# A short last row tile of an expert, packed by GpSimd and run with 16 matmuls

## The chip, the cores and the metric

The kernel runs on one core of a Trainium2 chip. The metric is the device time of one execution in microseconds, the median of several runs. A core has five engines with a queue each: TensorE (matmuls, "PE" in the profile), VectorE ("DVE"), ScalarE ("ACT"), GpSimd ("POOL") and SyncE ("SP", which here only issues DMAs). They meet through semaphores.

## The reference

Chunked attention with memory tokens, then a mixture of experts over its output. Only the second half matters here:

```python
# x: (3072, 512), the attention's output; E = 8 experts, F = 1024, capacity = 768
logits = x @ w_gate
expert_idx = np.argmax(logits, axis=1)
gate_w = softmax(logits)[np.arange(N), expert_idx]
# rows of an expert, in order, up to the capacity
h = np.maximum(np.einsum('ecd,edf->ecf', disp, w1), 0.0)   # layer 1
y = np.einsum('ecf,efd->ecd', h, w2)                       # layer 2
out[i] = gate_w[i] * y[expert_idx[i], pos[i]]
```

Each row goes to one expert. With the inputs drawn here the eight experts get 529, 195, 426, 381, 565, 320, 162 and 494 rows. All arrays are float32.

## The kernel before

**Stages.** The attention runs first, over 24 tiles of 128 tokens. While it runs, the routing gives each token a slot in a DRAM table `x_d`, sorted by expert, and scatters the token's row there (512 values, its gate weight in column `D`, its token number in column `D + 1`). After it the experts run one after the other, in `expert(e)`, L933.

**Precision.** A float32 matmul is done as three matmuls in the fast format float32r: each operand is split into a part `hi` and a rest `lo`, and hi x hi, hi x lo and lo x hi are added in PSUM. So weights (`w1`, `w2`), rows (`x`) and the hidden layer (`h`) each exist twice. The splits are an ACT copy (`hi`) and a DVE subtraction (`lo`).

**Tiles of rows.** An expert has up to six tiles of 128 rows. Tiles 0 and 1 (`TA = 2` of them, "early" tiles) are used only by an expert with more than 512 rows (`big`), and by expert 0, whose first 256 rows are computed ahead while the routing ends. Tiles 2 to 5 (`TB = 4`) hold the other rows: tile `TA`, that is 2, always runs; tiles 3, 4 and 5 run if the count of rows says so. `m32` is the count in units of 32 rows, without the early ones. The counts are known only on the chip: engines load them into registers (`values`, L795) and branch with `tc.If`.

**One expert**, in the order in which each engine's queue has it:

1. SP: `load_x(e + 1)` (L813) loads the next expert's rows from `x_d` to `xg`, under a Switch over the number of tiles.
2. Layer 1 (`layer1`, L876): one of six variants by width, the next of which is announced by `hint`. TensorE fills PSUM banks `p1[0..3]` in turn, with 12 matmuls for each of 8 `f`; `relu` (L870) makes `hhi` on ACT and `hlo` on DVE. Between, `split2` splits w2, and SP then loads the next expert's `w2` (L957).
3. Layer 2 of tile `TA` on TensorE: `mm2` (L909), for each of 8 `f` three matmuls of 128x512, 24 in all. Among them stand the transposes of the next expert's rows (`trans_x`, L831).
4. `split1(3)`: three of the eight splits of the next expert's `w1`; then `put_y` (L914) of tile `TA`: DVE scales the PSUM bank by the gate weights into a buffer `y`, of which there are three in turn, and GpSimd issues an indirect DMA that scatters the 128 rows into the output.
5. `trans_a(e + 1)`, tiles 0 and 1 if the expert is big, and tiles 3, 4 and 5 under an If each (L982). Between them stand the other five splits of w1. An If that is not taken does one tiny matmul on TensorE instead (`instead`, L865).
6. SP: the load of `w1` of expert `e + 2` (L988) into `raw1`, once the eight splits have read it. The next expert's `load_x` stands behind it on SP's queue.

PSUM has eight banks: `p1[0..3]`, two more of `p2`, and two for the transposes. Layer 2 takes the banks by `order` (L764): tile 2 the first of `p2`, tile 0 the second, and tiles 1, 3, 4, 5 the banks `p1[0]` to `p1[3]`.

Of the kernel before, what the change touches and what calls it, by code (L numbers as in the profile page):

```python
# [10 lines left out]
I32 = mybir.dt.int32  # L11
# [39 lines left out]
class Kernel:  # L51
# [7 lines left out]
    def run(self):  # L59
        tc, nc = self.tc, self.nc  # L60
        with ExitStack() as ctx:
            wp = ctx.enter_context(tc.tile_pool(name="wp", bufs=1))
            dr = ctx.enter_context(tc.tile_pool(name="dr", bufs=1, space=bass.MemoryType.DRAM))
            self.x_d = dr.tile([E * self.nt * P, XW], F32, name="x_d")
            self.ident = wp.tile([P, P], F32, name="ident")
            make_identity(nc, self.ident)
            self.w1hi = wp.tile([P, KD, F], F32R, name="w1hi")
            self.w1lo = wp.tile([P, KD, F], F32R, name="w1lo")
            self.raw1 = wp.tile([P, KD, F], F32, name="raw1")
            self.raw2 = wp.tile([P, KF, D], F32, name="raw2")  # L70
            self.pad = wp.tile([P, XW], F32, name="pad")
            nc.vector.memset(self.pad[:, 0:260], 0.0)
            nc.gpsimd.memset(self.pad[:, 260:], 0.0)
            nc.gpsimd.memset(self.pad[:, D + 1:D + 2], BIG)
            self.pads = wp.tile([P, E], I32, name="pads")
            self.zb = wp.tile([P, P], BF16, name="zb")

            self.big = wp.tile([1, E], I32, name="big")
            self.m32 = wp.tile([1, E], I32, name="m32")
            self.kind = wp.tile([1, E], I32, name="kind")  # L80
            self.wide = wp.tile([1, E], I32, name="wide")
            flags = wp.tile([1, 2], I32, name="flags")
            self.full, self.ok = flags[:, 0:1], flags[:, 1:2]
            with tc.manual_schedule(engines={ET.PE, ET.Activation, ET.DVE, ET.Pool, ET.SP}):
                self.attention()
                self.experts(ctx)
# [620 lines left out]
    def finish_routing(self):  # L707
# [26 lines left out]
        nc.vector.tensor_scalar(out=ci, in0=self.m32, scalar1=1.0, scalar2=-1.0, op0=ALU.max, op1=ALU.add)  # L734
        nc.vector.tensor_scalar(out=ci, in0=ci, scalar1=2, scalar2=None, op0=ALU.logical_shift_right)
        nc.vector.scalar_tensor_tensor(out=self.kind, in0=self.big, scalar=float(TB), in1=ci, op0=ALU.mult, op1=ALU.add)
# [7 lines left out]
        top = sm.tile([1, 1], F32, name="f_top")  # L744
# [4 lines left out]
    def experts(self, ctx):  # L749
# [9 lines left out]
        self.my = ctx.enter_context(tc.tile_pool(name="my", bufs=3, side="right"))  # L759
        p1 = ctx.enter_context(tc.tile_pool(name="p1", bufs=1, space=PSUM))  # L760
# [3 lines left out]
        self.order = [TA] + list(range(TA)) + list(range(TA + 1, TA + TB))  # L764
# [14 lines left out]
        self.rows = self.values(self.kind, ET.SP, 3 * TB)  # L779
        self.load_x(0)  # L780
# [65 lines left out]
    def trans_a(self, e):  # L846
        with self.tc.If(self.a[e] > 0) as c:  # L847
            for d in range(0, KD, 2):
                self.trans_x(e, d, 2)
        self.instead(c, self.p2[1])  # L850
# [71 lines left out]

    def tokens(self, e, t0, t1):
# [4 lines left out]
    def layer2(self, e, t, tok):  # L928
        ps = self.p2[self.order.index(t)]
# [3 lines left out]
    def expert(self, e):  # L933
# [5 lines left out]
        if not e:  # L939
# [6 lines left out]
            ps = self.p2[self.order.index(TA - 1)]  # L946
# [18 lines left out]
        if e + 1 < E:  # L965
            self.hint(e + 1)

# [5 lines left out]
        self.put_y(e, self.p2[0], TA, tok)  # L973
        if e + 1 < E:
# [5 lines left out]
        self.instead(c, self.p2[1])  # L980
        split1(2)
        for t in range(TA + 1, TA + TB):  # L982
            with tc.If(m > 4 * (t - TA)) as c:
                self.layer2(e, t, tok)
            self.instead(c, self.p2[self.order.index(t)])
# [31 lines left out]
```

## Time and profile before

| what | us |
|---|---|
| median of 3 runs | 504.53 (504.53, 510.5, 504.26) |
| the profiled execution | 508.52 |
| its span, first to last instruction | 506.7 |
| TensorE busy in the span | 461.3 |
| VectorE busy | 295.4 |
| ScalarE busy | 233.8 |
| GpSimd busy | 115.4 |
| mean granted TensorE clock | 0.977 |

The span falls into the attention, until about 150 us, the routing and early tiles, and the experts, from about 190 us to the end. TensorE is the busiest engine; matmuls overlap, so that a row's time can exceed the time from its start to the next one's. In the timelines below a row has its start, its time, engine, line, operation, the tiles written and read, and in brackets the idle time of the engine just before it and what ended that. "issue" in that place means that the profile shows no releaser. "SPq", "DVEq" and so on are the sequencers of the engines.

### The profile page before, as it was taken

The numbers are of one execution on the slowest core, as the hardware profiler recorded it, in microseconds if no ns is written. First come the engines' busy times: TensorE is split into PE (matmuls) and PEld (weight loads), VectorE is DVE, ScalarE is ACT, GpSimd is POOL, SyncE is SP. The second block draws the span as 40 slices with busy tenths as digits, with TensorE's granted clock in tenths as the row PEclk, the third lists the DMA queues.
The fourth block names the chain that finished last, engine by engine and source line by source line (L and its number), as shares of the span: only waits on it lengthen the run. The fifth ranks groups of instructions, "written<-read, shape, count | busy, mean of one in ns | idle before, by whom it ended". The sixth has DMA issues, their size and how long they took to land.

```text
span 506.7 us, 11689 instructions
## 1 busy us (share of the span) xinstructions
PE 461.3 (91%) x4317; PEld 394.1 (78%) x4317; DVE 295.4 (58%) x678; ACT 233.8 (46%) x462; POOL 115.4 (23%) x151
## 2 busy tenths in 40 slices
PE   7889988998868599898999999999999999889993
PEld 6778776777558579787888899799988989767782
DVE  6899797999854723456555525726442565554410
ACT  6799778888432413325434314524330553433300
POOL 8531133554623370020100210010022011020011
PEclk9999999999997899999999999999999999989997
DMA  9697899974672585227472480543321644630010
GB/s 212 152 213 157 198 272 261 208 200 104 134 273 93 177 303 169 108 70 266 160 243 61 156 294 15 190 154 125 125 87 50 217 172 167 225 115 2 4 41 38
DMA packets 77816, 78.71 MB, mean 155 GB/s; under 512 B 31762, under 2 KB 58510, under 8 KB 77648
## 3 DMA queue, kind: packets, MB, share of 16 engines
q1 hardware_dynamic: 72848, 61.93, 42.6%
q0 software_dynamic: 4800, 14.95, 7.7%
q8 instruction: 55, 0.90, 0.8%
q14 instruction: 113, 0.93, 0.6%
HBM read 60.86 MB, written 15.99 MB: 152 GB/s over the span
## 4 chain that ended last, share of the span: by engine, by line
issue 37%; DMA 34%; PE 16%; DVE 7%; ACT 2%; SPq 2%; POOLq 1%; DVEq 0%; POOL 0%; ACTq 0%
DMA out_dram<-y,tok 27%; DMA x_d<-pad,pads 4%; PE ps L509 3%; PE ps L463 3%; PE ps L550 3%; PE ps L533 2%; ACT kw L480 2%; DVE vw L415 1%; PE ps L332 1%; PE ps L475 1%; PE ps L603 1%; DMA raw<-in_q_dram 1%; DMA vw<-in_v_dram 1%; SPq L397 1%; DMA xg<-x_d 1%
## 5 line engine op out<-in xcount | busy, mean ns | idle before, releaser
L912 PE MATMUL p<-w2hi,hhi 128*128 128x512 f32 x224 | 92.7, 414 | 6.5 <-ACT w2hi L854 5.1
L872 ACT ACTIVATE hhi<-p 128x384 fp32r<-128x384 f32 (+2 forms) x68 | 33.7, 497 | 140.2 <-PE p L863 118.1
L919 POOL DMA_INDIRECT out_dram<-y,tok x28 | 32.0, 1144 | 279.1 <-DVEq L847 142.3
L912 PE MATMUL p<-w2lo,hhi 128*128 128x512 f32 x224 | 89.1, 398 | 0.0
L912 PE MATMUL p<-w2hi,hlo 128*128 128x512 f32 x224 | 88.7, 396 | 0.0
L873 DVE SCALAR_TENSOR_TENSOR hlo<-p,hhi 128x384 fp32r<-128x384 f32 (+2 forms) x68 | 37.6, 564 | 70.6 <-ACT hhi L872 47.0
L863 PE MATMUL p<-xhi,w1hi 128*128 128x256 f32 (+5 forms) x288 | 57.6, 322 | 4.1 <-issue 2.5
L863 PE MATMUL p<-xlo,w1hi 128*128 128x256 f32 (+5 forms) x288 | 57.2, 321 | 0.0
L863 PE MATMUL p<-xhi,w1lo 128*128 128x256 f32 (+5 forms) x288 | 57.1, 321 | 0.0
L912 PEld LDWEIGHTS p<-w2hi,hhi 128*128 128x128 f32 x224 | 42.9, 191 | 15.0 <-ACT w2hi L854 5.3
L918 DVE TENSOR_SCALAR y<-p,xg 128x512 f32<-128x512 f32 x28 | 21.0, 749 | 56.7 <-PE p L912 33.9
L912 PEld LDWEIGHTS p<-w2hi,hlo 128*128 128x128 f32 x224 | 42.7, 191 | 10.1
L863 PEld LDWEIGHTS p<-xhi,w1hi 128*128 128x128 f32 x288 | 45.3, 189 | 6.7 <-issue 3.2
L912 PEld LDWEIGHTS p<-w2lo,hhi 128*128 128x128 f32 x224 | 42.9, 192 | 7.8
L863 PEld LDWEIGHTS p<-xlo,w1hi 128*128 128x128 f32 x288 | 46.2, 190 | 2.1
L863 PEld LDWEIGHTS p<-xhi,w1lo 128*128 128x128 f32 x288 | 46.0, 189 | 2.0
L843 ACT CAST xhi<-px 128x512 fp32r<-128x512 f32 x34 | 19.8, 587 | 49.4 <-PE px L839 28.2
L855 DVE TENSOR_TENSOR w2lo<-raw,w2hi 128x512 fp32r<-128x512 f32 x64 | 41.2, 687 | 0.7
L480 ACT COPY kw<-ps 64x256 f32<-64x256 f32 x92 | 35.7, 388 | 10.8 <-PE ps L475 9.6
L844 DVE TENSOR_TENSOR xlo<-px,xhi 128x512 fp32r<-128x512 f32 x34 | 23.4, 691 | 28.1 <-ACT xhi L843 23.7
L829 DVE TENSOR_TENSOR w1lo<-raw,w1hi 128x512 fp32r<-128x512 f32 x56 | 36.6, 686 | 2.5 <-ACT w1hi L828 1.3
L550 PE MATMUL ps<-vw,pT 128*32 128x130 f32 x768 | 29.4, 277 | 8.4 <-issue 4.7
(156 smaller groups left out, 712.9 us busy)
## 6 DMA issues: line engine op xcount, KB each, us to landing
raw<-in_moe_w_dram SPq DMA_DIRECT2D x16, 2048.0 KB
raw<-in_q_dram SPq DMA_DIRECT2D x11, 512.0 KB
raw<-in_k_dram SPq DMA_DIRECT2D x10, 512.0 KB
vw<-in_v_dram SPq DMA_DIRECT2D x57, 64.0 KB
xg<-x_d SPq DMA_DIRECT2D x3, 792.0 KB
vw<-in_v_dram SPq DMA_DIRECT2D x31, 72.0 KB
xg<-x_d SPq DMA_DIRECT2D x4, 528.0 KB
xg<-x_d SPq DMA_DIRECT2D x2, 1056.0 KB
```

The costliest lines, as they stand in the source:

```text
L480: (nc.vector.tensor_copy if n == 0 and i else nc.scalar.copy)(out=kw[r, 2 * i:2 * i + 2, :, hf, 24 + j:56:2], in_=ps[j * 64:j * 64 + 64, h ...
L550: nc.tensor.matmul(ps[32 * c4:32 * c4 + 32, i * 130:i * 130 + 130], pT[:, pr * P + 32 * c4:pr * P + 32 * c4 + 32], vw[:, c + c4 + 1, :, pr ...
L829: (eng or self.nc.vector).tensor_tensor(out=lo[sl], in0=raw[sl], in1=hi[sl].bitcast(F32), op=ALU.subtract)
L843: nc.scalar.copy(out=self.xhi[:, d:d + k, sl], in_=pv)
L844: nc.vector.tensor_tensor(out=self.xlo[:, d:d + k, sl], in0=pv, in1=self.xhi[:, d:d + k, sl].bitcast(F32), op=ALU.subtract)
L855: self.nc.vector.tensor_tensor(out=self.w2b[j // 4][:, j % 4], in0=self.raw2[:, j], in1=self.w2a[:, j].bitcast(F32), op=ALU.subtract)
L863: self.nc.tensor.matmul(ps, a[:, d, fs], b[:, d, o:o + w], start=(i + d == 0), stop=(i == 2 and d == KD - 1))
L872: self.nc.scalar.activation(out=self.hhi[hs], in_=ps, func=AF.Relu)
L873: self.nc.vector.scalar_tensor_tensor(out=self.hlo[hs], in0=ps, scalar=0.0, in1=self.hhi[hs].bitcast(F32), op0=ALU.max, op1=ALU.subtract)
L912: self.nc.tensor.matmul(ps, a[:, f, t * P:t * P + P], b, start=(f == 0 and i == 0), stop=(f == KF - 1 and i == 2))
L918: nc.vector.tensor_scalar(out=y, in0=ps, scalar1=self.xg[e % 2][:, t, D:D + 1], scalar2=None, op0=ALU.mult)
L919: nc.gpsimd.indirect_dma_start(out=self.out[:, :], out_offset=bass.IndirectOffsetOnAxis(ap=tok[:, t:t + 1], axis=0), in_=y, in_offset=None ...
```

## The change

A tile is *short* if it is the last one of tiles 3, 4 and 5 in use and holds at most 64 rows (counted in units of 32). A new array `last`, worked out beside `m32` in the routing, holds its number (1 to 3 for tiles 3 to 5) or 0, and PE, DVE and GpSimd load it into registers. With it:

- `pack`, on GpSimd, after layer 1 and ahead of tile `TA`'s scatter: it copies `hhi` of the 64 rows to the first 64 columns of the place of tile 5, and `hlo` of the same rows to the next 64 columns; the gate weights twice, and the token numbers. A nest of Ifs picks the tile.
- `layer2_short`, right behind tile `TA`: 128 packed columns against `w2a` (hi) and `w2b` (lo), 16 matmuls in place of 24. DVE scales the lower half into `z`, then the upper half and adds `z` to it; GpSimd scatters 64 rows.
- Tiles 3 to 5 run in their old place only if they have more than 64 rows, and the unpacked tile's Ifs stay.
- Banks: tiles 0, 1, 3, 4 get `p1[0]`, `p1[1]`, `p1[2]`, `p1[3]`, tiles 2 and 5 the first of `p2`, the short tile the second. The matmul of an untaken If goes to `p1[0]`.
- `top` in the routing takes the place of a dead row, which spares some memory.

```diff
+            self.last = wp.tile([1, E], I32, name="last")
...
         nc.vector.tensor_scalar(out=ci, in0=self.m32, scalar1=1.0, scalar2=-1.0, op0=ALU.max, op1=ALU.add)
+        left = late
+        nc.vector.tensor_scalar(out=left, in0=ci, scalar1=3, scalar2=None, op0=ALU.bitwise_and)
+        nc.vector.tensor_scalar(out=left, in0=left, scalar1=2.0, scalar2=None, op0=ALU.is_lt)
         nc.vector.tensor_scalar(out=ci, in0=ci, scalar1=2, scalar2=None, op0=ALU.logical_shift_right)
+        nc.vector.tensor_tensor(out=self.last, in0=ci, in1=left, op=ALU.mult)
...
-        self.order = [TA] + list(range(TA)) + list(range(TA + 1, TA + TB))
+        self.bank = [2, 3, 0, 4, 5, 0]
...
+        self.short = self.values(self.last, ENGS, TB)
...
+    def pack(self, e):
+
+        n, h, s = self.short[e], P // 2, (TA + TB - 1) * P
+        st, sg = self.my.tile([P, 1], I32, name="stok", bufs=2), self.my.tile([P, 1], F32, name="sgate", bufs=2)
+        xg, copy = self.xg[e % 2], self.nc.gpsimd.tensor_copy
+
+        def go(k):
+            if k < TB - 1:
+                with self.tc.If(n > k) as c:
+                    go(k + 1)
+                with c.Else():
+                    move(TA + k)
+            else:
+                move(TA + k)
+
+        def move(t):
+            if t * P < s:
+                copy(out=self.hhi[:, :, s:s + h], in_=self.hhi[:, :, t * P:t * P + h].bitcast(F32))
+            copy(out=self.hhi[:, :, s + h:s + P], in_=self.hlo[:, :, t * P:t * P + h].bitcast(F32))
+            for r in (0, h):
+                copy(out=sg[r:r + h, :], in_=xg[0:h, t, D:D + 1])
+            copy(out=st[0:h, :], in_=xg[0:h, t, D + 1:D + 2])
+
+        with self.tc.If(n > 0):
+            go(1)
+        return st, sg
+
+    def layer2_short(self, e, st, sg):
+
+        nc, h, s, ps = self.nc, P // 2, (TA + TB - 1) * P, self.p2[1]
+        for f in range(KF):
+            for i, b in enumerate((self.w2a[:, f], self.w2b[f // 4][:, f % 4])):
+                nc.tensor.matmul(ps, self.hhi[:, f, s:s + P], b, start=(f == 0 and i == 0), stop=(f == KF - 1 and i == 1))
+        y, z = self.my.tile([P, D], F32, name="y"), self.z
+        nc.vector.tensor_scalar(out=z, in0=ps[h:P, :], scalar1=sg[h:P, :], scalar2=None, op0=ALU.mult)
+        nc.vector.scalar_tensor_tensor(out=y[0:h, :], in0=ps[0:h, :], scalar=sg[0:h, :], in1=z, op0=ALU.mult, op1=ALU.add)
+        nc.gpsimd.indirect_dma_start(
+            out=self.out[:, :], out_offset=bass.IndirectOffsetOnAxis(ap=st[0:h, :], axis=0),
+            in_=y[0:h, :], in_offset=None, bounds_check=NTOK - 1, oob_is_err=False)
...
         if e + 1 < E:
             self.hint(e + 1)
+        st, sg = self.pack(e)
...
         self.put_y(e, self.p2[0], TA, tok)
+        with tc.If(self.short[e] > 0) as c:
+            self.layer2_short(e, st, sg)
+        self.instead(c, self.p2[2])
         if e + 1 < E:
             self.trans_a(e + 1)
...
         for t in range(TA + 1, TA + TB):
-            with tc.If(m > 4 * (t - TA)) as c:
+            with tc.If(m > 4 * (t - TA) + 2) as c:
                 self.layer2(e, t, tok)
-            self.instead(c, self.p2[self.order.index(t)])
+            self.instead(c, self.p2[2])
             split1(1)
```

More of the change, by code (lines that the diff above doesn't have):

```diff
@@ L742, in finish_routing @@
             nc.vector.scalar_tensor_tensor(out=self.wide, in0=self.m32, scalar=float(w // 32), in1=self.wide, op0=ALU.is_gt, op1=ALU.add)
-        top = sm.tile([1, 1], F32, name="f_top")
+        top = late[:, 0:1]
         nc.vector.tensor_reduce(out=top, in_=n[0:1, :], axis=AX.X, op=ALU.max)
@@ L759, in experts @@
         self.my = ctx.enter_context(tc.tile_pool(name="my", bufs=3, side="right"))
+        self.z = mr.tile([P // 2, D], F32, name="z")
         p1 = ctx.enter_context(tc.tile_pool(name="p1", bufs=1, space=PSUM))
@@ L849, in trans_a @@
                 self.trans_x(e, d, 2)
-        self.instead(c, self.p2[1])
+        self.instead(c, self.p2[2])
     def split2(self, todo):
@@ L928, in layer2 @@
     def layer2(self, e, t, tok):
-        ps = self.p2[self.order.index(t)]
+        ps = self.p2[self.bank[t]]
         self.mm2(ps, t, range(KF))
@@ L945, in expert @@
                     self.layer2(e, t, tok)
-            ps = self.p2[self.order.index(TA - 1)]
+            ps = self.p2[self.bank[TA - 1]]
             for i, fs in enumerate((range(0, 3), range(3, 6), range(6, KF))):
@@ L979, in expert @@
                 self.layer2(e, t, tok)
-        self.instead(c, self.p2[1])
+        self.instead(c, self.p2[2])
         split1(2)
         for t in range(TA + 1, TA + TB):
-            with tc.If(m > 4 * (t - TA)) as c:
+            with tc.If(m > 4 * (t - TA) + 2) as c:
                 self.layer2(e, t, tok)
-            self.instead(c, self.p2[self.order.index(t)])
+            self.instead(c, self.p2[2])
             split1(1)
```

## The prediction, before the changed kernel was timed

> **What bounds the kernel now.** I read the page's head first, then the TensorE timeline of the expert stage, then the list of what TensorE waited for, then the DVE, GpSimd and SyncE timelines around each wait.
>
> ```profile
> span 506.7 us, 11689 instructions
> PE 461.3 (91%) x4317; PEld 394.1 (78%) x4317; DVE 295.4 (58%) x678; ACT 233.8 (46%) x462; POOL 115.4 (23%) x151
> 212.69 0.19 PE L868 MATMUL p<-zb 128*128 128x2 bf16 x2
> 223.89 0.18 PE L868 MATMUL p<-zb 128*128 128x2 bf16 x1
> 223.93 0.73 PE L863 MATMUL p<-xhi,w1hi 128*128 128x256 f32 x4
> 239.38 0.63 PE L839 MATMUL px<-ident,xg 128*128 128x128 f32 x4 [2.42 <-issue]
> 254.07 1.05 PE L863 MATMUL p<-xhi,w1hi 128*128 128x448 f32 x4 [0.31 <-DVE y L918]
> 437.50 0.63 PE L839 MATMUL px<-ident,xg 128*128 128x128 f32 x4 [1.52 <-issue]
> 451.86 1.16 PE L863 MATMUL p<-xhi,w1hi 128*128 128x512 f32 x4 [2.51 <-issue]
> ```
>
> Inside the expert stage TensorE runs nearly without holes. Between the two L868 markers at 212.69 and 223.89 lie two layer 2 tiles of expert 0, 48 matmuls in 11.20 us: 0.233 us each (the 0.4 us "busy" of one overlaps its neighbours). The marker itself, the matmul of an If not taken, costs 0.04 us (223.89 to 223.93). So TensorE sets the time, except in four places of the expert stage shown above. Two of them, 2.42 us in expert 1 and 1.52 us in expert 6, matter here. They are the first transposes of the *next* expert's rows: the wait is for a load.
>
> ```profile
> 225.47 0.37 SPq L988 DMA_DIRECT2D raw<-in_moe_w_dram  x1
> 232.71 0.37 SPq L825 DMA_DIRECT2D xg<-x_d  x1
> 424.50 0.37 SPq L988 DMA_DIRECT2D raw<-in_moe_w_dram  x1
> 431.61 0.37 SPq L825 DMA_DIRECT2D xg<-x_d  x1
> 237.00:238.00 1.00, 0.00 (x0) 0.00 (x0) 0.89 (x2) 0.09 (x1) 0.00 (x0) 1.00 0.35 124
> 238.00:239.00 1.00, 0.00 (x0) 0.00 (x0) 0.00 (x0) 0.00 (x0) 0.00 (x0) 1.00 0.08 31
> ```
>
> The last two rows are windows in expert 1 (their last two columns are the DMA share and GB/s): the DMA engines run dry while TensorE idles, and then it starts. The row load is issued 7.2 us (225.47 to 232.71) and 7.1 us (424.50 to 431.61) after the weight load w1 on the same queue, and TensorE starts 13.9 us (225.47 to 239.38) and 13.0 us (424.50 to 437.50) after that weight load. So in these two experts the clock of everything is the moment at which SyncE may issue L988, and that is when the eighth split of w1 has been done on DVE.
>
> ```profile
> 215.91 0.75 DVE L918 TENSOR_SCALAR y<-p,xg 128x512 f32<-128x512 f32 x1
> 216.94 1.42 POOL L919 DMA_INDIRECT out_dram<-y,tok  x1 [9.38 <-DVEq L847]
> 220.60 0.75 DVE L918 TENSOR_SCALAR y<-p,xg 128x512 f32<-128x512 f32 x1 [1.26 <-DMA out_dram<-y,tok]
> 221.27 0.68 DVE L829 TENSOR_TENSOR w1lo<-raw,w1hi 128x512 fp32r<-128x512 f32 x1
> 224.09 0.75 DVE L918 TENSOR_SCALAR y<-p,xg 128x512 f32<-128x512 f32 x1 [2.13 <-PE p L868]
> 224.76 0.68 DVE L829 TENSOR_TENSOR w1lo<-raw,w1hi 128x512 fp32r<-128x512 f32 x1
> 216.94 3.54 DMA out_dram<-y,tok
> 371.32 3.33 DMA out_dram<-y,tok
> 375.43 0.97 POOL L919 DMA_INDIRECT out_dram<-y,tok  x1 [2.69 <-DMA out_dram<-y,tok]
> 206.59 2.69 DMA out_dram<-y,tok
> ```
>
> This is expert 0, whose tiles are TA, t3 and t4 (TA+1, TA+2 are called t3, t4 here). The second output tile of DVE (220.60) waits until the first one's scatter has landed (216.94 + 3.54 = 220.48): three buffers y go round, and t3 comes three allocations after TA. And GpSimd's second scatter of a chain (375.43, expert 4) waits until the first has landed (371.32 + 3.33 = 374.65), and starts 0.78 us later: scatters to the output go one at a time.
>
> **The change part by part.**
>
> *Fewer matmuls.* By the reference's counts (529, 195, 426, 381, 565, 320, 162, 494 rows) the last tile has 64 rows or fewer in experts 0, 2, 4, 5 and 6. Each replaces 24 matmuls by 16: 8 x 0.233 = 1.87 us, in all 9.33 us, every one on TensorE's path. In experts 1, 3 and 7 nothing is saved.
>
> *The pack on GpSimd.* Two copies of 128x512 (one in expert 2) and three of 64x1.
>
> ```profile
> L829 POOL TENSOR_TENSOR w1lo<-raw,w1hi 128x512 fp32r<-128x512 f32 x8 | 10.5, 1307 | 17.8 <-ACT w1hi L828 17.8
> L496 POOL COPY kw<-kw 64x672 f32<-64x672 f32 x10 | 7.4, 739 | 40.5 <-ACT kw L480 17.9 <-PE ps L642 9.0 <-DVE m L517 7.4
> L542 POOL COPY xr<-tok 128x1 f32<-128x1 f32 x24 | 5.5, 240 | 0.2
> 405.02 0.56 DVE L873 SCALAR_TENSOR_TENSOR hlo<-p,hhi 128x384 fp32r<-128x384 f32 x1 [1.20 <-ACT hhi L872]
> 411.73 0.19 PE L868 MATMUL p<-zb 128*128 128x2 bf16 x2
> ```
>
> A copy of 672 elements takes 739 ns, the two-input operation on 512 takes 1307 ns: 0.6 to 1.3 us each, so 1.2 to 2.6 us for both; the three small ones at 240 ns (0.7 us) follow them, and TensorE doesn't need them. In expert 5 the last hlo ends at 405.58, tile TA's matmuls at 411.73: 6.1 us of cover, and GpSimd is idle then. I cost it at nothing; without cover it would be 2.6 us. In expert 0 GpSimd is held until 206.59 + 0.97 by an early scatter, and TA ends at 212.69: 5.1 us of cover. The Trainium skill ("SBUF — State Buffer", section on who interferes with whom) adds that a GpSimd operation reading SBUF and a DVE operation with two SBUF inputs lock each other out for a whole instruction; as an estimate by that page the two copies could each wait for one DVE split (0.68 us above), 4.0 us in all and still under cover, and nothing in this trace shows such a wait.
>
> *DVE.* A short tile takes two operations (z, y) of about 0.75 us in place of one. DVE is at 58%, so this costs nothing by itself. But they stand on DVE's queue ahead of five splits of w1, and they wait for TensorE's short tile.
>
> *Scatters and buffers: what is queued behind.* Now y is taken by TA, short, t0, t1, t3: t3 comes three after *short*. In expert 0, from TA's end at 212.69: y(TA) ends at 216.66, its scatter is issued at 216.94 and lands at 220.48. The short tile's matmuls end at 216.4, z and y by 218.3, but its scatter starts only 0.78 us after that landing, 221.26, and lands after 2.69 to 3.54 us (the extremes above; I take 3.1, the middle), at 224.36. TensorE has finished t3 at 212.69 + 40 x 0.233 = 222.0, but y(t3) starts at 224.48; then come 0.67 to the next operation, split seven (0.68), 0.16 of branch and split eight (0.68): L988 at 226.7. It was 225.47. So although TensorE is 1.87 us ahead, the loads are 1.2 us *later*, and expert 1's transposes start 1.2 us later than now. Expert 5 is alike:
>
> ```profile
> 414.95 0.75 DVE L918 TENSOR_SCALAR y<-p,xg 128x512 f32<-128x512 f32 x1
> 415.98 3.18 DMA out_dram<-y,tok
> ```
>
> landing 419.16, short's scatter 419.94 to 423.04, y(t3) 423.17, L988 at 425.4 in place of 424.50: 0.9 us later. The price is (1.87 + 1.2) + (1.87 + 0.9) = 5.84 us. With the quickest scatters it is 5.0, with the slowest 6.7; without the buffer wait 1.9. In experts 2, 4 and 6 no such load is in the way: 4 ends in t3, whose buffer is long free because t0 and t1 lie between; 2 has t4 after t3 and 17 us of layer 1 behind it; 6 loads nothing more.
>
> *The clock.* The two waits grow to 2.42 + 3.07 = 5.5 us and 1.52 + 2.77 = 4.3 us.
>
> ```profile
> 237.85:241.27 3.42, 1.90 (x11) 1.62 (x12) 0.82 (x3) 0.59 (x1) 0.00 (x0) 1.00 0.57 163
> 449.48:452.89 3.41, 1.03 (x5) 0.89 (x6) 1.29 (x3) 0.00 (x0) 0.01 (x1) 1.00 0.23 84
> 452.89:456.30 3.41, 3.41 (x10) 2.65 (x9) 1.01 (x2) 0.00 (x0) 1.16 (x1) 0.50 0.06 23
> ```
>
> Windows of 3.41 us, the granted clock in the third column from the end: a window in which TensorE was busy for 1.90 us did no harm, one with 1.03 us was followed by 3.41 us at half clock, a loss of 1.7 us. A hole of 4.3 us leaves, whatever its place, a window with at most 1.3 us of work, nearer to the second. I take 1.7 us for each: 3.4 us; the bounds are 0 and two windows each, 6.8.
>
> *Banks.* t3 moves from the bank that layer 1's second f uses to that of its third: the 0.31 us at 254.07 goes.
>
> *Small things.* Eight more untaken Ifs on TensorE at 0.04 us: 0.3. Eight more register values on TensorE, DVE and GpSimd:
>
> ```profile
> 177.09 1.09 DVE L773 MEMSET p<- 128x256 f32 x4
> 179.80 0.17 DVE L925 CAST tok<-xg 128x2 int32<-128x2 f32 x1 [1.62 <-issue]
> 165.68 0.35 DVE L735 TENSOR_SCALAR f_ci<-f_ci 1x8 int32<-1x8 int32 x1
> 171.49 0.43 DVE L343 SCALAR_TENSOR_TENSOR hlo<-ps,hhi 128x256 fp32r<-128x256 f32 x1 [2.69 <-ACT hhi L342]
> ```
>
> 33 values are loaded within 1.62 us, so 8 take at most 0.4; I count it all. Three more DVE operations in the routing, at most 0.35 us each, vanish in the 2.69 us for which DVE then waits anyway.
>
> *Sum:* -9.33 + 5.84 + 3.4 - 0.31 + 0.3 + 0.4 = +0.3 us. The profiled execution took 508.52 us (span 506.7), 4 us above the median of the runs shown, 504.53; I put the difference on the median: 504.8 us.
>
> **The rivals.** *Everything arrives.* If the scatters or buffers don't hold the splits (by a quicker landing, or because y(t3) needn't wait), 9.33 us less 0.3 for the small things: 495.5 us. Against it stand 220.60 and 375.43, which show both waits. *Late loads, no clock loss:* 504.8 - 3.4 = 501.4; for it, that 2.42 us of idle in expert 1 cost no clock.
>
> *New stalls at branches (slower).* TensorE's hole of 2.51 us at 451.86 stands at the jump into expert 7's widest layer 1, followed by the half clock: 4.2 us together. After the change expert 6 jumps over five blocks in a row there, and seven other places get one more jump. One new hole gives 509, three give 517.4 (over 2%). Against it: the jump at 223.89 cost 0.04 us. The Trainium skill ("Runtime: NRT & Kernel Launch", section on instruction fetch) says that a taken branch out of the loaded pages must wait for a fetch; by that rule each new jump may be such a hole, and this trace agrees at one of them and not at the others.
>
> *The pack is late:* if GpSimd's branches and copies outlast TA by up to 1.5 us in all five, 7.5 us: 512; against it, 5.1 to 6.1 us of cover.
>
> **How the numbers follow.** Likeliest case 45% (its own range 500.5 to 508), late loads without clock loss 20%, everything arrives 13%, new stalls 14%, late pack 8%. The range 495.5 to 511 takes in the second and the edge of the third and one new stall. A change of 2%, 10.1 us, is about what can be told from none: faster needs more than all 9.33 us, 0.05; slower needs three new stalls, 0.06; same 0.89.
>
> **What would show it.** Right: L988 of expert 0 about 14.0 us after TA's end in place of 12.8; holes of 4 to 6 us ahead of L839 in experts 1 and 6, with half clock behind them; y(t3) waiting on the scatter in experts 0 and 5; experts 2, 4 and 6 shorter by 1.9 us. Wrong: no longer holes there, or a hole ahead of the short tile's first matmul, or new holes at L868.

## The result, and the profile after

The changed kernel takes 513.15 us (median of 20 runs, 507.6 to 520.05), the kernel before 505.21 us (20 runs, 499.83 to 510.5): the ratio is 1.0137, 95% interval 1.0109 to 1.0166. It is slower, by less than 2%, and by more than the range allowed for (495.5 to 511). The profiled execution of the changed kernel took 513.91 us, 5.4 us more than the one of before. The latter lay 3.3 us above its median and the former 0.8 us, which makes up the difference to the 7.9 us between the medians.

From the page of the changed kernel, its span and busy times:

```profile
span 511.9 us, 11827 instructions
PE 455.1 (89%) x4285; PEld 389.0 (76%) x4285; DVE 299.6 (59%) x686; ACT 233.2 (46%) x462; POOL 124.6 (24%) x175
```

TensorE has 32 instructions and 6.2 us of work less (461.3 before), and yet the span is 5.2 us longer: the gain turned into idle time. All lines of the code behind the new functions have moved: layer 1 is L870 now, the marker of an untaken If L875, layer 2 L919, the short tile L962, the transposes L846, the w1 load L1039. The timeline of TensorE, the short tile's first and last matmul and the rows with idle time in the experts 0, 1, 5 and 6:

```profile
209.23 0.79 PE L919 MATMUL p<-w2hi,hhi 128*128 128x512 f32 x1 [3.07 <-issue]
...
217.93 0.48 PE L962 MATMUL p<-w2hi,hhi 128*128 128x512 f32 x1
...
221.73 0.20 PE L875 MATMUL p<-zb 128*128 128x2 bf16 x2
...
244.72 0.63 PE L846 MATMUL px<-ident,xg 128*128 128x128 f32 x4 [3.21 <-issue]
...
258.17 1.05 PE L870 MATMUL p<-xhi,w1hi 128*128 128x448 f32 x4 [1.59 <-DVE y L925]
...
440.30 0.63 PE L846 MATMUL px<-ident,xg 128*128 128x128 f32 x4 [1.64 <-issue]
449.96 0.20 PE L875 MATMUL p<-zb 128*128 128x2 bf16 x2
452.81 0.16 PE L875 MATMUL p<-zb 128*128 128x2 bf16 x1 [2.65 <-DVEq L1028]
453.45 0.16 PE L875 MATMUL p<-zb 128*128 128x2 bf16 x1 [0.47 <-issue]
453.86 0.16 PE L875 MATMUL p<-zb 128*128 128x2 bf16 x1 [0.25 <-issue]
456.64 2.04 PE L870 MATMUL p<-xhi,w1hi 128*128 128x512 f32 x4 [2.61 <-DVEq L1034]
```

The short tile itself works: 16 matmuls from 217.93 to 221.73, 3.80 us. New are two places. Expert 0 idles for 3.07 us ahead of tile TA (1.44 before). At the end of expert 6 the markers, which ran back to back before, wait 2.65 us for DVE, and the jump into expert 7's layer 1 still idles for 2.61 us behind that (2.51 before). The same two places in the kernel before, where layer 2 is L912 and the marker L868:

```profile
205.28 0.49 PE L912 MATMUL p<-w2hi,hhi 128*128 128x512 f32 x1 [1.44 <-ACTq L901]
...
449.14 0.20 PE L868 MATMUL p<-zb 128*128 128x2 bf16 x2
```

The windows of the changed kernel, on the clock's own grid of 3.41 us (the granted clock is the third column from the end):

```profile
205.36:208.77 3.41, 0.81 (x7) 0.64 (x6) 1.04 (x3) 0.49 (x1) 0.00 (x0) 1.00 0.58 217
208.77:212.19 3.42, 2.96 (x8) 2.27 (x9) 0.00 (x0) 0.00 (x0) 2.63 (x6) 0.50 0.20 77
...
239.48:242.90 3.42, 2.03 (x12) 1.43 (x10) 2.20 (x5) 1.41 (x3) 0.00 (x0) 1.00 0.84 302
242.90:246.31 3.41, 1.59 (x9) 1.44 (x10) 0.48 (x2) 0.59 (x1) 0.00 (x0) 1.00 0.22 69
246.31:249.72 3.41, 3.41 (x20) 2.85 (x20) 1.14 (x3) 1.18 (x2) 0.00 (x0) 1.00 0.98 338
...
451.12:454.53 3.41, 0.49 (x3) 0.19 (x2) 2.94 (x5) 0.28 (x1) 0.40 (x2) 1.00 0.23 84
454.53:457.94 3.41, 1.30 (x3) 1.14 (x4) 1.09 (x2) 0.00 (x0) 1.19 (x1) 0.50 0.11 28
457.94:461.36 3.42, 3.42 (x9) 2.65 (x9) 0.00 (x0) 0.00 (x0) 0.00 (x0) 0.50 0.01 2
```

The new hole of expert 0 brings a window at half clock, that of expert 6 two (one before). The hole of 3.21 us ahead of expert 1's transposes lies across two windows, which keep 2.03 and 1.59 us of work, and costs no clock. DVE's timeline of the changed kernel, two rows of expert 0 and three of expert 6:

```profile
222.81 0.74 DVE L965 SCALAR_TENSOR_TENSOR y<-p,sgate,z 64x512 f32<-64x512 f32 x1
228.91 0.75 DVE L925 TENSOR_SCALAR y<-p,xg 128x512 f32<-128x512 f32 x1 [3.08 <-DMA out_dram<-y,stok]
...
451.04 0.74 DVE L965 SCALAR_TENSOR_TENSOR y<-p,sgate,z 64x512 f32<-64x512 f32 x1
451.95 0.69 DVE L836 TENSOR_TENSOR w1lo<-raw,w1hi 128x512 fp32r<-128x512 f32 x1 [0.17 <-DVEq L854]
452.80 1.29 DVE L836 TENSOR_TENSOR w1lo<-raw,w1hi 128x512 fp32r<-128x512 f32 x2 [0.15 <-DVEq L1028]
```

GpSimd's, the pack of expert 0 and the scatters of tile TA and of the short tile:

```profile
209.96 0.63 POOL L947 CAST hhi<-hhi 128x512 fp32r<-128x512 f32 x1
210.52 0.62 POOL L948 CAST hhi<-hlo 128x512 fp32r<-128x512 f32 x1
...
211.56 0.18 POOL L951 CAST stok<-xg 64x1 int32<-64x1 f32 x1
222.77 0.98 POOL L926 DMA_INDIRECT out_dram<-y,tok  x1 [11.03 <-DVE z L964]
226.58 0.92 POOL L966 DMA_INDIRECT out_dram<-y,stok  x1 [2.82 <-DVE w1lo L836]
```

SyncE's queue, the w1 loads in the experts 0 and 5:

```profile
231.13 0.37 SPq L1039 DMA_DIRECT2D raw<-in_moe_w_dram  x1
...
427.74 0.37 SPq L1039 DMA_DIRECT2D raw<-in_moe_w_dram  x1
```

The pack ends at 211.74, 6.2 us ahead of the short tile. y(t3) waits for the short tile's scatter, as forecast. The w1 load is issued 13.2 us after TA's end (217.93) in place of 12.8. And in expert 6 DVE passes the If of tiles 0 and 1 (L1028) at 452.80, when the short tile's z and y and a split are done: at that moment TensorE's marker is let go.

The next table cuts the experts into stages, by the first and last rows of layer 1 (L1) and the 24th matmul of tile TA in each TensorE timeline; "tail" is from TA's end to the next expert's layer 1. The changed kernel was profiled twice more, beside later experiments. The last five rows are experiments, told below: "own banks" are the markers' banks as before, "late" puts the short tile behind tiles 3 to 5, and "free bank" gives the markers a bank that nothing has read for long.

| profiled execution, us | e0: L1 + TA | e0 tail to e1's TA end | e2 tail | TA of e2, e4, e5 | e4 tail | e5 tail to e6's TA end | e6 tail | e7: L1 |
|---|---|---|---|---|---|---|---|---|
| before | 21.6 | 32.6 | 17.2 | 6.8, 6.7, 6.8 | 22.7 | 31.7 | 8.8 | 24.3 |
| after | 25.4 | 32.6 | 15.4 | 7.1, 6.9, 7.1 | 20.9 | 31.2 | 10.8 | 25.0 |
| after, second | 24.0 | 31.8 | 15.4 | 7.1, 7.0, 7.1 | 20.9 | 34.1 | 10.8 | 25.4 |
| after, third | 26.5 | 33.9 | 15.4 | 7.1, 6.9, 7.1 | 20.9 | 33.8 | 11.0 | 25.6 |
| own banks | 25.4 | 36.2 | 15.4 | 7.1, 7.0, 7.1 | 20.9 | 34.1 | 7.0 | 24.4 |
| pack's Ifs on GpSimd alone | 24.2 | 33.6 | 15.4 | 6.9, 6.7, 6.8 | 20.9 | 31.5 | 11.4 | 25.4 |
| the same, second | 20.1 | 33.2 | 15.4 | 6.8, 6.7, 6.9 | 21.0 | 31.3 | 11.9 | 25.3 |
| late, own banks | 26.4 | 30.7 | 15.5 | 7.1, 6.9, 7.0 | 21.0 | 30.3 | 10.1 | 22.8 |
| late, free bank, GpSimd alone | 20.1 | 30.2 | 15.4 | 6.8, 6.7, 6.8 | 21.0 | 28.6 | 9.7 | 22.8 |

### The profile page after: what moved, and what is told of

Its sections match the earlier page's. It is cut to its first block, busy times and chain, and to the rows that moved or that the text cites. A ratio compares the mean times of both kernels' runs of the same rounds, so it can differ in the third digit from the quotient of the medians.

```text
span 511.9 us, 11827 instructions
## 1 busy us (share of the span) xinstructions
PE 455.1 (89%) x4285; PEld 389.0 (76%) x4285; DVE 299.6 (59%) x686; ACT 233.2 (46%) x462; POOL 124.6 (24%) x175
## 5 line engine op out<-in xcount | busy, mean ns | idle before, releaser
L879 ACT ACTIVATE hhi<-p 128x384 fp32r<-128x384 f32 (+2 forms) x68 | 33.8, 498 | 139.3 <-PE p L870 112.8
L919 PE MATMUL p<-w2hi,hhi 128*128 128x512 f32 x184 | 77.0, 418 | 9.0 <-DVE p L779 6.0
L919 PE MATMUL p<-w2lo,hhi 128*128 128x512 f32 x184 | 73.7, 400 | 0.0
L919 PE MATMUL p<-w2hi,hlo 128*128 128x512 f32 x184 | 73.5, 400 | 0.0
L926 POOL DMA_INDIRECT out_dram<-y,tok x23 | 23.7, 1031 | 197.0 <-DVEq L1022 82.5
L870 PE MATMUL p<-xhi,w1hi 128*128 128x256 f32 (+5 forms) x288 | 58.3, 325 | 7.8 <-DVEq L1034 2.6
L870 PE MATMUL p<-xhi,w1lo 128*128 128x256 f32 (+5 forms) x288 | 57.0, 320 | 0.0
L870 PE MATMUL p<-xlo,w1hi 128*128 128x256 f32 (+5 forms) x288 | 56.7, 319 | 0.0
L870 PEld LDWEIGHTS p<-xhi,w1hi 128*128 128x128 f32 x288 | 45.6, 190 | 10.4 <-issue 6.4
L870 PEld LDWEIGHTS p<-xlo,w1hi 128*128 128x128 f32 x288 | 46.1, 190 | 2.1
L870 PEld LDWEIGHTS p<-xhi,w1lo 128*128 128x128 f32 x288 | 46.1, 190 | 2.1
L919 PEld LDWEIGHTS p<-w2hi,hhi 128*128 128x128 f32 x184 | 35.5, 193 | 16.0 <-issue 9.3
L925 DVE TENSOR_SCALAR y<-p,xg 128x512 f32<-128x512 f32 x23 | 17.2, 749 | 50.8 <-PE p L919 29.2
L862 DVE TENSOR_TENSOR w2lo<-raw,w2hi 128x512 fp32r<-128x512 f32 x64 | 42.8, 711 | 0.6
L919 PEld LDWEIGHTS p<-w2hi,hlo 128*128 128x128 f32 x184 | 35.4, 192 | 8.2
L919 PEld LDWEIGHTS p<-w2lo,hhi 128*128 128x128 f32 x184 | 35.5, 193 | 6.4
```

The source lines that it names most:

```text
L862: self.nc.vector.tensor_tensor(out=self.w2b[j // 4][:, j % 4], in0=self.raw2[:, j], in1=self.w2a[:, j].bitcast(F32), op=ALU.subtract)
L870: self.nc.tensor.matmul(ps, a[:, d, fs], b[:, d, o:o + w], start=(i + d == 0), stop=(i == 2 and d == KD - 1))
L879: self.nc.scalar.activation(out=self.hhi[hs], in_=ps, func=AF.Relu)
L919: self.nc.tensor.matmul(ps, a[:, f, t * P:t * P + P], b, start=(f == 0 and i == 0), stop=(f == KF - 1 and i == 2))
L925: nc.vector.tensor_scalar(out=y, in0=ps, scalar1=self.xg[e % 2][:, t, D:D + 1], scalar2=None, op0=ALU.mult)
L926: nc.gpsimd.indirect_dma_start(out=self.out[:, :], out_offset=bass.IndirectOffsetOnAxis(ap=tok[:, t:t + 1], axis=0), in_=y, in_offset=None ...
```

## The experiments

Chips differ (the kernel before took 504.4 to 506.2 us in four of the five sets of experiments, 513.38 us in the set of the first four runs), so each ratio is to the kernel before on the same chip; brackets hold the 95% interval. In two sets the changed kernel ran again beside its variants; that run is called the mark. All kernels compute the whole reference.

**Is it the bank of the markers?** In the changed kernel the marker of an untaken If of tiles 3 to 5 writes `p1[0]`, the bank that tile 0 also uses and DVE reads in the If of tiles 0 and 1. The first experiment gives the kernel before the new banks and markers and nothing else:

```diff
-        self.order = [TA] + list(range(TA)) + list(range(TA + 1, TA + TB))
+        self.bank = [2, 3, 0, 4, 5, 0]
...
-            self.instead(c, self.p2[self.order.index(t)])
+            self.instead(c, self.p2[2])
```

> The kernel before with the new bank map alone, and the untaken Ifs' matmul into p1[0]; no short tile. If the banks or that matmul cost by themselves (TensorE then waits at an untaken If for DVE to pass the If of tiles 0 and 1), this is slower than before by 1 to 3 us, with a wait on DVE at L868 at the end of expert 6. If not, it is at 0 to -0.3 us (the bank wait in expert 2 goes).

Measured: 1.0056 [1.0011, 1.0101], slower by 2.9 us in the ratio, but without the sign named: in its profile the markers at expert 6's end run back to back, and 3.45 us of idle stand behind them, at the jump into expert 7's layer 1. The second gives the changed kernel the markers' own banks back, once in the set of the first experiment and once beside a mark:

```diff
-            self.instead(c, self.p2[2])
+            self.instead(c, self.p2[self.bank[t]])
             split1(1)
```

> The changed kernel, where the untaken Ifs of tiles 3 to 5 do their tiny matmul in the tile's own bank. If TensorE's wait of 2.65 us at the end of expert 6 comes from that matmul sharing a bank with tile 0's output, it goes from there; the layer 1 matmul behind it shares the same bank, so that 1 to 3 us come back unless the fetch hides them: 511 to 513 against 513.2. If the fetch is the cause, no difference.

> The changed kernel again, as the mark for the three that run on the same chip. 1.014 to 1.019 times the kernel before.

> The matmul of an untaken If of tiles 3 to 5 goes to the bank of that tile again and no longer to tile 0's; the short tile stays right behind tile TA. Theory 'placeholder bank' (TensorE is held at that matmul because DVE must first reach the same If): expert 6's end loses its 2.65 us hole and the half clock behind it, 4 to 6 us under the mark, ratio to before 1.005. Rival 'place' (the short tile in that place holds DVE and the loads, whatever the bank): at most 1.5 us under the mark.

Measured: 1.0055 [1.0016, 1.0094] in the first set; in the other the mark is 1.0194 [1.0151, 1.0237] and own banks 1.0079 [1.0045, 1.0114], medians 516.39 and 510.34 us. TensorE's timeline with own banks at expert 6's end:

```profile
454.33 0.39 PE L962 MATMUL p<-w2lo,hhi 128*128 128x512 f32 x1
454.56 0.53 PE L875 MATMUL p<-zb 128*128 128x2 bf16 x5
457.45 1.52 PE L870 MATMUL p<-xhi,w1hi 128*128 128x512 f32 x4 [2.35 <-DVEq L1028]
```

All five markers run at once again, and the table's tail of expert 6 is 7.0 us: 1.8 us under before, just what the spared matmuls are worth, where the mark has 11.0. The theory holds: by the medians 6 us of the loss go with this bank. In the profiles 4.0 us go in this tail and 1.2 in expert 7's layer 1. Expert 1's tail falls too, to 6.3 us, where the changed kernel's three profiles have 8.0, 8.4 and 7.2 and the kernel before 6.2.

One stage got longer. From expert 0's tail to the end of expert 1's TA both profiles with own banks took 36.2 and 36.3 us, more than any profile of the changed kernel (31.8 to 33.9). From the profile in the table:

```profile
230.85 0.75 DVE L925 TENSOR_SCALAR y<-p,xg 128x512 f32<-128x512 f32 x1 [5.06 <-DMA out_dram<-y,stok]
233.07 0.37 SPq L1039 DMA_DIRECT2D raw<-in_moe_w_dram  x1
246.74 1.09 PE L846 MATMUL px<-ident,xg 128*128 128x128 f32 x4 [4.89 <-issue]
...
243.03:246.44 3.41, 0.00 (x0) 0.00 (x0) 0.00 (x0) 0.00 (x0) 0.00 (x0) 1.00 0.46 175
246.44:249.85 3.41, 3.11 (x10) 2.66 (x11) 0.86 (x2) 0.59 (x1) 0.00 (x0) 0.50 0.54 166
```

Here y(t3) waits until 4.30 us after the start of the short tile's scatter (226.55), the w1 load is issued 15.2 us after TA's end (217.88), and TensorE idles for 4.89 us ahead of the transposes, with half clock behind: what the prediction had described for the changed kernel. Why the scatter lands later with own banks is not known.

**Is it the place?** The short tile's block goes behind tiles 3 to 5, with the markers' bank as changed, and with own banks:

```diff
         self.put_y(e, self.p2[0], TA, tok)
-        with tc.If(self.short[e] > 0) as c:
-            self.layer2_short(e, st, sg)
-        self.instead(c, self.p2[2])
...
             split1(1)
+        with tc.If(self.short[e] > 0) as c:
+            self.layer2_short(e, st, sg)
+        self.instead(c, self.p2[2])
         if e + 2 < E:
```

> The short tile's block stands behind tiles 3 to 5, and the matmul of an untaken If still goes to tile 0's bank. Theory 'place': 5 to 8 us under the mark. Theory 'placeholder bank': DVE reaches the Ifs sooner now, as the short tile's two operations are behind them, so that part of the hole goes too, but expert 5's end and expert 6's keep one of 1 us or more each: 2 to 4 us under the mark, 3 us or more above the earlier run with both edits (which was 1.003 times before).

> The changed kernel once more, beside before on this chip, since before takes 8 us more on the second chip than on the first. 1.0 to 1.5% over before is expected by every theory; it is the mark for the three others.

> The changed kernel with the short tile behind tiles 3 to 5 (the place where the full tile stood before), and untaken Ifs in the tile's own bank. The 16 matmuls and the pack stay. If the place right behind TA is the cause (DVE's queue held by the short tile, tile 3's output waiting for two scatters, TensorE waiting for DVE at untaken Ifs), this is 8 to 10 us under the changed kernel and 1 to 4 us under before. If the new code itself or the pack costs, it stays near the changed kernel.

Measured: late alone 1.0126 [1.008, 1.0172], 3.8 us under the mark's median of 516.39; late with own banks 1.0028 [0.9991, 1.0064] beside a mark of 1.0193 [1.0147, 1.024] (more than had been expected of it), 506.26 against 514.64 us. The two causes together make up the whole loss of 8 us against the kernel before, but the 1 to 4 us under it did not come, and the 9.33 us of spared matmuls do not show in the time. How much is the place's alone is less sure: own banks without it stood at 1.0079, on another chip, and the intervals overlap; late alone gained no more than the theory of the bank had said. What the place costs is in the table: with the short tile last, the stretches from expert 0 to 1 and from 5 to 6 take 30.7 and 30.3 us where the changed kernel has 31.8 to 33.9 and 31.2 to 34.1. The w1 load, which waits for the last split of w1, is then issued 10.0 and 9.9 us after TA's end, in place of 13.2 and 12.8 in the changed kernel, since z, y and the scatter no longer stand ahead of the splits. Expert 7's layer 1 (22.8) begins right behind 16 matmuls. Against that, 3.44 us of idle stand ahead of expert 0's tile TA, and the fifth marker of expert 6 waits for 3.85 us:

```profile
448.27 0.16 PE L875 MATMUL p<-zb 128*128 128x2 bf16 x1 [3.85 <-DVEq L854]
```

**Is it the chain of scatters, or the late splits?** In one run the output scatters are declared independent, so that they don't wait for one another; in another the last five splits of w1 stand together ahead of tile 3:

```diff
-        nc.gpsimd.indirect_dma_start(
+        i = nc.gpsimd.indirect_dma_start(
...
+        self.tc.declare_no_dep(i.ins, group="outs", reason="each token has a row of its own")
+        self.tc.add_to_no_dep_group("outs", i.ins)
```

```diff
-        split1(1)
         with tc.If(a > 0) as c:
...
-        split1(2)
+        split1(5)
...
-            split1(1)
```

> The changed kernel, where the scatters into the output don't wait for one another (each writes rows of its own). The short tile's scatter is then issued 1.5 us behind TA's and tile 3's output no longer waits: w1's load 1 to 2 us earlier in experts 0 and 5. If the chain of scatters is the cause of the late loads, 2 to 5 us under the changed kernel; if the place of the splits and the fetches are, under 1 us.

> The changed kernel, where the last five splits of the next w1 stand together behind tiles 0 and 1 and ahead of tiles 3 to 5, so that none of them waits behind y of tile 3. If the late row loads cost (w1's load is held by the eighth split, and the row load stands behind it), w1's load is issued about 9 us after TA's end in place of 13, the holes ahead of the transposes in experts 1 and 6 (3.2 and 1.6 us in the profile) go with the half clock that sometimes follows them, and this is 4 to 8 us under the changed kernel. If instruction fetches at the Switch are the cause, no difference beyond 1 us.

Measured: 1.0147 [1.0092, 1.0202] and 1.0204 [1.0152, 1.0255], the mark 1.0193. Free scatters took y(t3)'s wait for a DMA away and are 2.1 us faster by the medians, but the intervals overlap, so that a gain is not shown; early splits gain nothing: expert 1's layer 1 then waits 3.58 us for DVE, with half clock behind.

**Is it the code itself?** In one run no tile is ever short, so all the new Ifs stand there untaken; in one the hint of the next layer 1 moves behind tiles 0 and 1.

```diff
-        nc.vector.tensor_tensor(out=self.last, in0=ci, in1=left, op=ALU.mult)
+        nc.vector.scalar_tensor_tensor(out=self.last, in0=ci, scalar=0.0, in1=left, op0=ALU.mult, op1=ALU.mult)
...
-            with tc.If(m > 4 * (t - TA) + 2) as c:
+            with tc.If(m > 4 * (t - TA)) as c:
```

> The changed kernel with no tile ever short: last is multiplied by 0, and tiles 3 to 5 run by the old bound. All new code is there, and jumped over. If the code's mere length costs (the page of the next layer 1 that the hint has fetched is displaced before the Switch, so that the Switch's branch waits for a fetch), this is slower than before by 3 to 8 us, with holes of 1 to 2.6 us at the first layer 1 matmul of several experts. If the loss of the change lies in late loads, buffers and clock, this is within 1 us of before.

> The changed kernel with the hint for the next layer 1 moved from ahead of tile TA to behind tiles 0 and 1, nearer to the Switch. If the holes at the start of layer 1 are fetches of a page that was announced too early, they go in experts 0, 1, 5 and 6 (1.0 + 1.6 + 0.85 + 2.6 us in the profile, and some clock): 506 to 509. If they are waits for DVE, it stays at 513; if a hint so late comes too late, it is slower.

Measured: 0.9972 [0.9939, 1.0005] and 1.0100 [1.0054, 1.0146]. Untaken, the new code costs nothing that can be measured, although the markers write `p1[0]` here too: the wait needs the short tile's work on DVE as well. Since this run has the new banks and markers too, they don't explain by themselves why the first experiment lost 0.6%; that stays open. With the moved hint expert 0's hole fell to 0.8 us, but the loss stayed.

**Is it the pack's Ifs on TensorE?** `self.short` is held in registers of TensorE, DVE and GpSimd, so all three run the pack's nest of Ifs. With a register of GpSimd's own they don't:

```diff
+        self.shortp = self.values(self.last, ET.Pool, TB)
...
-        n, h, s = self.short[e], P // 2, (TA + TB - 1) * P
+        n, h, s = self.shortp[e], P // 2, (TA + TB - 1) * P
```

> The pack's nest of Ifs asks a register that GpSimd alone holds, so TensorE and DVE no longer run its branches; eight more values are loaded by GpSimd. Theory 'branches of the pack on TensorE': the hole between layer 1 and tile TA in expert 0 goes from 3.1 us to 2 or less, and 1 us in each of the experts 0, 3, 4 and 5 where TensorE is not ahead of its work, 2 to 4 us under the mark. Rival 'TensorE's sequencer is ahead there': within 1 us of the mark.

> The changed kernel with the pack's Ifs on GpSimd alone, again, since its first six runs lay in two groups (509 to 511 and 517 to 521). Theory 'branches of the pack on TensorE': a ratio to the kernel before of 1.010 to 1.014 (the changed kernel: 1.014 to 1.019). Rival 'TensorE's sequencer is ahead there': 1.014 or more.

Measured: first 517.08 us, median of six runs from 508.82 to 521.2, beside the mark of 516.39; then 1.0199 [1.0132, 1.0265]. In the time, nothing, as the rival said. In the profiles, TA of the experts 2, 4 and 5 goes from 7.1, 6.9, 7.1 back to 6.8, 6.7 and 6.8 or 6.9: the nest does cost 0.2 to 0.3 us each time on TensorE. Expert 0's L1 and TA took 24.2 us in one execution and 20.1 in the other of the same kernel, so its hole isn't set by the nest alone. Nor does the nest always bring it: in the profile with early splits, whose code is the changed kernel's up to there, this stage took 20.1 us, with no hole ahead of TA.

**Is there a version that beats both?** Late, own banks, and the pack's Ifs on GpSimd alone; then free scatters too; then the moved hint too:

> Three edits at once: short tile behind tiles 3 to 5, untaken Ifs in their own banks, and the pack's Ifs on GpSimd alone. The first two alone stood at 1.003 times the kernel before. Theory 'the pack's branches on TensorE cost time in expert 0': its hole ahead of tile TA goes from 3.4 us to 2 or less and the half clock behind it goes too, 2 to 4 us: 0.995 to 0.999. Rival 'TensorE's hole there is the fetch of the code behind the Switch, which stays': 1.003 again.

> The run with three edits, and output scatters that don't wait for each other. Theory 'late loads through the chain of scatters': another 2 us, as from the changed kernel, 0.991 to 0.995. Rival: with the short tile last there is no scatter of it ahead of y(t3), so nothing is left to gain: the same as the run with three edits within 0.003.

> The same four edits, and the hint of the next layer 1 moved from ahead of tile TA to behind tiles 0 and 1. If the hole ahead of TA in expert 0 is the fetch of code that the hint's own fetch stands ahead of, it falls under 1 us (it was 0.8 us in the earlier run with the moved hint) and the time by another 1 to 3 us; against it, less time for the hinted code to arrive by the next layer 1: 1 us more in each of experts 1 and 6.

Measured: 1.0004 [0.996, 1.0048], 1.0147 [1.0072, 1.0221] and 1.0137 [1.0077, 1.0197]. The first lies between the theory's range and the rival's 1.003, and its interval reaches both. Free scatters cost here: in the second of the three, DVE waits in expert 2's short tile and at the next jump, and expert 3's layer 1 takes 22 us in place of 17. From its list of waits in that stretch (total us, times, longest):

```profile
DVE hlo L881 <- issue: 5.1, 1, 5.1
DVE y L968 <- DMA out_dram<-y,tok: 4.6, 1, 4.6
```

Why the scatters landed that late was not tried. In the first of the three a marker still waits at expert 6's end; tile 5's own bank is tile TA's, which DVE reads in between:

```profile
436.80 0.24 PE L876 MATMUL p<-zb 128*128 128x2 bf16 x4
442.21 0.16 PE L876 MATMUL p<-zb 128*128 128x2 bf16 x1 [5.16 <-DVEq L1026]
```

So the last two runs give all these markers the short tile's bank, unread since the expert before, without and with the GpSimd register:

```diff
...
-            self.instead(c, self.p2[2])
+            self.instead(c, self.p2[1])
             split1(1)
+        with tc.If(self.short[e] > 0) as c:
+            self.layer2_short(e, st, sg)
+        self.instead(c, self.p2[1])
```

> The short tile behind tiles 3 to 5, and every untaken If of those tiles and of the short tile writes the short tile's own bank, which nothing has read since the last expert's end. In the earlier runs with the tiles' own banks tile 5's bank is tile TA's, and that matmul waited 3.9 to 5.2 us for DVE at expert 6's end, with half clock behind. Theory 'placeholder bank': that hole goes too, 3 to 5 us from the earlier 1.003: ratio 0.993 to 0.997. Rival: the wait moves to the short tile's code or to the next layer 1, and the ratio stays at 1.003.

> The same, with the pack's Ifs on GpSimd alone. Theory 'the pack's branches on TensorE and DVE': expert 0's hole ahead of tile TA under 2 us and 1 to 3 us less time than the run without this edit on the same chip: 0.987 to 0.993. Rival 'not on the path': the two runs within 0.003 of each other.

Measured: 0.9999 [0.9964, 1.0033] and 0.9966 [0.9931, 1.0001]; medians 505.11 and 503.29 us, before 504.37. The second run's gain of 1.8 us over the first lies within the intervals, so the GpSimd register is not shown to gain. The profiles show more: the wait for DVE is gone, but not the idle time, so the rival named for the first of the two had the mechanism, and the bank was not what set the idle time at this marker when the short tile stands last. In the first run the fifth marker stands about as long as before, now without a releaser:

```profile
445.82 0.19 PE L875 MATMUL p<-zb 128*128 128x2 bf16 x1 [4.37 <-issue]
```

In the second:

```profile
433.53 0.27 PE L876 MATMUL p<-zb 128*128 128x2 bf16 x5
...
434.45 0.39 PE L963 MATMUL p<-w2lo,hhi 128*128 128x512 f32 x1
438.70 0.58 PE L963 MATMUL p<-w2hi,hhi 128*128 128x512 f32 x1 [3.86 <-issue]
```

This is the last kernel: the markers run at once, four matmuls of the short tile too, and then TensorE stands for 3.86 us in the middle of 16 matmuls for which the profile shows no wait. No version is faster than the kernel before by more than its interval. The stages of its profile show what the change could give (expert 0 to 1 2.4 us and 5 to 6 3.1 us under before), but that execution, of 498.17 us, was the fastest of its twelve.

## Why the prediction was wrong

The forecast was +0.3 us; it came to +7.9.

**Fewer matmuls: right.** 3.80 us for 16. The tails of the experts 2 and 4 fell by 1.8 us each, as forecast (1.87).

**Banks and small things: the step that failed.** The prediction booked the new bank map as a gain of 0.31 us and eight untaken Ifs at 0.04 us each, from a marker that ran unhindered. But the change also sent the markers to `p1[0]`, the bank of tile 0, and put two DVE operations of the short tile ahead of DVE's If over tiles 0 and 1. The marker, which has no use but to keep the bank's order, so had to wait for DVE. Expert 6's tail grew by 2.0 us (10.8 for 8.8) where 1.87 less was forecast, and expert 7's layer 1 by 0.7 through another half-clock window: 4.6 us missed in one place. Expert 1's tail grew by 1.8. New holes at the marker's line were among the prediction's own signs of being wrong. The rival "new stalls at branches", at 14%, had the sign and the size (one hole 509, three 517.4 us), but its mechanism, code fetched at a jump, is not this one: own banks alone remove the wait, and 6 us with it.

**The pack at nothing: right on GpSimd, wrong for TensorE.** The copies (0.62 and 0.63 us in expert 0) ended 6.2 us ahead of the short tile. But the step counted the branches on GpSimd alone; TensorE and DVE run them too. Shown are 0.2 to 0.3 us in each of three experts. Expert 0 lost 2.4 to 4.9 us in L1 and TA in the three profiles; the hole there was 1.44 us long before, and isn't among the four places that the prediction lists. Why it is longer stays open: the two executions without the nest disagree, and so do executions of the same code (20.1 to 26.5 us).

**Scatters and buffers: the mechanism right, the size too large.** y(t3) waits for the short scatter as forecast. That started 8.65 us after TA's end (8.57 forecast), but had landed by 228.91, within 2.33 us, where 3.1 was taken from the scatters of 128 rows. So L1039 came 13.2 us after TA's end (forecast 14.0, before 12.8), and in expert 5 at 427.74, 12.8 us after the end of its TA, as before. In the profiled execution the two stretches cost 0.0 and -0.5 us in place of 2.9 and 2.6. The load can come later than forecast, too: with own banks the scatter took 1.9 us longer, L1039 came at 15.2 and 15.1 us in the two profiles, and the stretch from expert 0 cost 3.6 us, more than the 2.9 forecast.

**The clock: the rule right, the places wrong.** In the profile of after the holes ahead of the transposes were 3.21 and 1.64 us, not 5.5 and 4.3, and brought no half clock. In the second and third profile the stretch from expert 5 to 6 took 2.4 and 2.1 us more than before, close to the 2.6 forecast, with half clock behind holes of 3.24 and 2.81 us. From the third:

```profile
438.12:441.53 3.41, 0.60 (x6) 0.47 (x5) 1.71 (x3) 0.28 (x1) 1.95 (x4) 1.00 0.28 100
441.53:444.94 3.41, 3.41 (x13) 2.73 (x11) 0.70 (x2) 0.59 (x1) 0.00 (x0) 0.50 0.81 252
```

The Trainium skill ("TensorE: Matmul & The Clock Gate", part on HAM oscillation) warns of idle gaps over some 3.4 us; here half clock followed a gap of 2.81 us, whose window kept 0.60 us of work, and not one of 3.21 us across two windows. The half clock that did come stood mostly at expert 0's TA and at expert 7's layer 1, where the prediction had none to add. The clocks of all runs show the loss too: the mean granted clock was 0.961 in the median run of the changed kernel, and 0.973 to 0.974 in those of the kernel before in the five sets. As an estimate from these clocks and the spans, that is about 7 us of clock more withheld, where the forecast had 3.4; the part of it that falls on idle time costs nothing.

The sum of the errors in the profiled execution fits: expert 0's L1 and TA +3.8, expert 6's tail +3.9 and expert 7's layer 1 +0.7, expert 1's tail +1.8 (the layer 1 behind it waits 1.59 us for DVE's y, at 258.17, a wait that own banks remove too), an expert stage that starts 1.1 us later than allowed for, TA of three experts +0.7, against 6.0 of late loads and clock that didn't come in the two stretches and 1.1 us less than forecast in expert 2's layer 1: 4.9 us, by which the spans differ more than forecast (5.2 less 0.3); smaller differences cancel. Of the +3.8 in expert 0, and of the later start, the cause is open. The range missed because it was built on loads and clock, with the banks and the pack at values near nothing and no bounds of their own.

## What to carry to other kernels

A tiny instruction that only keeps an order is priced by what it must wait for: when its output buffer changes, list the last reader of the new buffer on every engine and where that engine will be by then. A branch on a register runs on every engine that holds the register, so a branch for one engine's work is better on a register of that engine alone (here 0.2 to 0.3 us in a stage, too little to show in the time). And work moved ahead on one queue is late for everything behind it: here the same 16 matmuls cost 8 us more in one place, and with one bank for the markers, than in another.

## What the runs showed of the hardware

On the grid of 3.41 us the twenty profiles of this case agree, between 185 and 500 us: a window at full clock with 1.46 us of TensorE work or less was followed by half clock each time, one with 1.67 us or more never; between 1.52 and 1.61 us both occur.

The hole of 3.86 us in the last kernel stands among matmuls for which the profile shows no wait. The DMA view of that kernel, from 436.1 to 437.3 us, in the middle of the hole, shows an instruction queue at work (packets, MB, share), and so does that of the run before it, from 442.9 to 444.4 us, in its marker's hole of 4.37 us (441.4 to 445.8):

```profile
q8 instruction: 1, 0.02, 5.8%
...
q8 instruction: 1, 0.02, 4.7%
```

That points to a fetch of code that TensorE had reached before it came; it was not tested apart. The Trainium skill ("Runtime: NRT & Kernel Launch", section on instruction fetch) has a crossing of a 16 KB boundary as mostly hidden; if these holes are such crossings, which no run tests, they were not hidden here, with 3.86 and 4.37 us and half clock behind. The same code stalled differently from execution to execution: ahead of expert 0's tile TA 1.99 us in one profile of the kernel with the GpSimd register, and none in the other.
